# A planned order for an attention, Fourier and feed-forward kernel: small copies on ScalarE's DMA queue, weights loaded and converted in pairs, and the planner's times replaced

## The chip, the cores and the metric

The kernel runs on one core of one Trainium2 chip. The metric is the device time of one execution in microseconds (us). The kernel before takes 1331.78 us, the median of three runs (1328.76 to 1334.36). Engines are named as in the profile: PE (TensorE), PEld (its weight loads), DVE (VectorE), ACT (ScalarE), POOL (GpSimd), SP (SyncE, which here only issues DMAs).

## What is computed

Eight batches of eight heads, 576 positions, head width 64, in float32:

```python
scores = q @ k.T / sqrt(64)                 # block-causal mask, blocks of 64
x = softmax(scores) @ v                     # heads side by side: [8, 576, 512]
u = x + real(fft(fft(x, axis=1), axis=2))   # over positions, then channels
un = (u - mean(u)) / sqrt(var(u) + 1e-6)
out = u + relu(un @ w_ch1) @ w_ch2          # 512 -> 2048 -> 512
```

The weights come as float64, handed over as the 64-bit integers that hold them: 32 rows of 128x512, 512 KB each.

## The kernel before

**Work per head.** Heads are numbered 0 to 63; heads 0 to 7 make batch 0. A head's raw q and k are loaded (`raw`, L288), rounded by ACT into a high part (`lead`, L291), and two DMAs copy parts of `lead` into another tile (`rest`, L295 and L296). DVE and POOL each compute half of the low part (`rest`, L302 and L304). PE then multiplies four pieces whose row maxima DVE reduces (`M`, L382 and L386, combined by L388). A transpose (L195), ACT (`mt`, L397) and a DMA of 2.5 KB (L399, `lead<-mt`) bring the maximum back as one more row of `lead`; this step is called the shift. Only after it landed can the scores run on PE (`rest` and `lead` with 73 rows). ACT takes two exponentials of each scores piece (`ph` L428, `p` L429) and POOL their difference (`pl`, L430). PE multiplies `ph` and `pl` with the two halves of V (`av`); DVE divides (`DEN`, `rec`, then `x` at L468). There is one `av` accumulator in all, so the next head's values wait for the `x` of this one. V arrives once for a pair of heads in a single buffer (`V`, L308), is summed by ACT (L317), and a small product with `ones` on PE (`vacc,ones`) and DVE and ACT split it (`VH` L333, `VL` L334).

**After a batch's eighth head** the results are written to DRAM (`xd`), read back partly mirrored (L529 to L532), folded by DVE (`tmp`, L543 and L544), transformed by 72 matmuls (with `fs`, `zc`, `zs`), normalised (L683 to L688), turned by PE, and then fed through the two weight matrices: 192 matmuls into `h` and 96 into `acc` for each of 18 pairs of pieces. These feed matmuls are most of PE's work and serve as filler between the attention steps of later batches.

**Weights.** Each of 32 rows of weights is loaded by SP (L803) into space of `W` that is not yet used, or into three tiles `u`; DVE makes float32 of it by three instructions of 128x512 (L812, L814, L816), ACT squares and sums (L818). When the sixteen rows of `w_ch1` are through, `weight_scale` finds a scale (a PE product with `ones` and `wst`), and `weight_parts` makes the two half-precision parts (ACT L840 and L843, POOL L844; for `w_ch2` ACT L840, DVE L846). Heads from 8 on may be planned only once the last row of weights has been converted (`"w32"`).

**The order.** `tile_attn_fourier_ffn` holds lanes of `Step`s and plans them with a small model of time: a step has a cost on PE and a chain of stays on the other engines (`"D0.65"` is 0.65 us of DVE, `"Q"` the SP queue, `"L"` a landing); `issue` books these on `Queue`s, adds `HOP` at each hand-over, and the next step emitted is one whose inputs the model calls ready. PE keeps the emitted order; the other engines' order is laid down by the framework when the program is built. Every engine then works strictly in its order.

Of the kernel before, what the change touches and what calls it, by code (L numbers as in the profile page):

```python
# [9 lines left out]
F32 = mybir.dt.float32  # L10
F32R = mybir.dt.float32r
F16 = mybir.dt.float16
# [20 lines left out]

HOP = 0.25
MARGIN = 0.3
AHEAD = (1.5, 6.0)
FREE = 0.5

PSHIFT = 5
# [112 lines left out]
class Queue:  # L152


    def __init__(self):
        self.taken = []

    def fit(self, t, cost):
# [18 lines left out]
def tile_attn_fourier_ffn(  # L177
# [67 lines left out]
    now = 0.0  # L245
    queues = {x: Queue() for x in "DAGQ"}
    done = {}
# [11 lines left out]
    def issue(step):  # L259
        nonlocal current, now  # L260
        t = max(now, ready(step))
        if step.cost:
            now = t = t + step.cost
            for x in queues.values():
                x.forget(now)
        free = None
        for engine, cost in step.chain:
            if engine == "B":
                free = t + HOP
            else:  # L270
                t = t + cost if engine == "L" else queues[engine].book(t + HOP, cost)
# [18 lines left out]
    def lead(h):  # L290
        nc.scalar.copy(LEAD[h % NB][0:D, 64:], raws[h])  # L291

    def lead_copies(h):
        x0, x1 = REST[h % NB].bitcast(F32), LEAD[h % NB].bitcast(F32)
        nc.sync.dma_start(x0[D:P, 0:S], x1[0:D, 64:64 + S])  # L295
        nc.sync.dma_start(x0[0:D, S:], x1[0:D, 64 + S:])  # L296

# [45 lines left out]
    def prepare_lane():  # L343
        for h in range(B * H):
# [3 lines left out]
            )  # L348
            yield Step(lambda: lead_copies(h), 0.0, ("Q1.2", "L2.2"), (("T", h),), ("TC", h), place=h - 0.9)
            yield Step(lambda: rest(h, 0), 0.0, (_d(S),), (("T", h),), ("T2", h, 0), place=h - 0.8)  # L350
# [41 lines left out]
    def shift(h):  # L392

        t = ps_tile()
        tp(t[0:5, 0:P], M[h % 2][:, 0:5], ident)
        mt = work.tile([5, P], F32R, name="mt", bufs=2)
        nc.scalar.activation(mt, t[0:5, 0:P], AF.Copy, bias=float(8.0 * PSHIFT * np.log(2.0)), scale=-1.0)  # L397
        dst = LEAD[h % NB][KM:KS, 0:640].rearrange("r (j p) -> r j p", j=5)
        nc.sync.dma_start(dst.bitcast(F32), mt.bitcast(F32))  # L399

# [87 lines left out]
    def max_lane():  # L488
        for h in range(B * H):
            for n in range(4):  # L490
# [3 lines left out]
                )  # L494
            yield Step(lambda: shift(h), 0.12, ("A0.26", "B", "Q0.6", "L2.2"), (("M", h),), ("X", h), True, place=h - 0.6)

# [281 lines left out]
    wsum = work.tile([P, NK, 2, P], F16, name="ul", bufs=2).rearrange("p c n d -> p (c n d)").bitcast(F32)  # L778
    wjunk = work.tile([P, DM], F32, name="left", bufs=2).bitcast(F16)[:, 0:DM]
    wst = work.tile([P, 8], F32, name="wst")  # L780

    def weight(i):

        if i < NF:
            return w1[P * (i % NK):P * (i % NK + 1), DM * (i // NK):DM * (i // NK + 1)]
        return w2[P * (i - NF):P * (i - NF + 1)]
# [5 lines left out]
    def raw(i):  # L792
        at = LANDS[i]
        t = stage[-1 - at].rearrange("p c d -> p (c d)") if at < 0 else W[:, at:at + 2].rearrange("p i x n -> p (i x n)")
        return t.bitcast(I32)

    loads = [0]

    def weight_loads(n):

        i = loads[0]
        while i < 2 * NF and LANDS[i] not in LANDS[n:i]:
            nc.sync.dma_start(raw(i), weight(i).bitcast(I32))  # L803
            i += 1
        loads[0] = i

    def weight_single(i):
        if loads[0] < i + 2:
            weight_loads(i)
        two = [(raw(j).rearrange("p (n x) -> p x n", x=2), W[:, j + 2].rearrange("p x n -> p (x n)").bitcast(I32)) for j in (i, i + 1)]  # L810
        for r, t in two:
            nc.vector.tensor_scalar(t, r[:, 1], 3, 0x3FFFFFFF, op0=ALU.logical_shift_left, op1=ALU.bitwise_and)  # L812
        for r, t in two:
            nc.vector.scalar_tensor_tensor(t, r[:, 0], 29, t, op0=ALU.logical_shift_right, op1=ALU.bitwise_or)  # L814
        for r, t in two:
            nc.vector.scalar_tensor_tensor(t, r[:, 1], -(1 << 30), t, op0=ALU.bitwise_and, op1=ALU.bitwise_or)  # L816
        for j, (r, t) in enumerate(two):
            nc.scalar.activation(wjunk, t.bitcast(F32), AF.Square, accum_out=wsum[:, i + j:i + j + 1])  # L818
        weight_loads(i)

# [27 lines left out]
    def weight_lane():  # L848
        yield Step(lambda: weight_loads(0), 0.0, ("Q5",), (("L", 0),), ("load",))
        def single(i):  # L850
            return Step(
                lambda: weight_single(i), 0.0, ("D0.5", "D0.5", "D0.82", "D0.82", "D0.85", "D0.85", "A0.82", "A0.82"), (("load",),),
                "w32" if i == 2 * NF - 2 else None,
            )
# [6 lines left out]

        for i in range(0, NF, 2):
            yield single(i)
        yield scale(0)
        for i in range(0, NF, 2):
            yield single(NF + i)
            yield parts(i)
            yield parts(i + 1)
        yield scale(1)
# [116 lines left out]
```

## Time and profile before

| what | us |
|---|---|
| median of three runs | 1331.78 |
| the profiled execution | 1330.52 |
| its span, first to last instruction | 1328.7 |
| PE busy in the span | 1190.9 |
| DVE / ACT / POOL busy | 701.5 / 573.0 / 526.6 |
| last `x` of batch 0 (head 7) starts on DVE at | 139.55 |
| first transform matmul of batch 0 at | 153.39 |

Times of the profile count from the start of the span; about 1.8 us of the profiled execution lie outside it. A busy engine need not be the one that sets the end: what matters is which engine has no idle time left in a stretch, and what the others wait for there.

### The profile page before, as it was taken

What the parts mean: (1) busy time and instruction counts of PE and PEld (TensorE: products, weight loads), DVE (VectorE), ACT (ScalarE), POOL (GpSimd) and SP (SyncE); (2) the same over time, 40 slices, a digit from 0 to 9 for tenths busy, and PEclk for the clock granted to TensorE, in tenths of its full rate; (3) what the DMA queues carried; (4) which work ended last, traced back from release to release, by engine and by line L of the source; (5) the groups of instructions that cost most, each with busy time, mean ns of one, the idle gap of its engine ahead of it and who ended that gap; (6) DMA issues with size and microseconds to landing.
All of it is one profiled execution on the core that took longest, in us unless ns stands there. A gap on an engine that the chain in (4) does not pass through costs nothing.

```text
span 1328.7 us, 25730 instructions
## 1 busy us (share of the span) xinstructions
PE 1190.9 (90%) x10068; PEld 890.2 (67%) x10068; DVE 701.5 (53%) x1626; ACT 573.0 (43%) x1309; POOL 526.6 (40%) x564
## 2 busy tenths in 40 slices
PE   3456469999998999899899899999999999999998
PEld 2455357777676777777677677777767667666665
DVE  6895477465656645764444764567433433312221
ACT  4566566554545454545455645554322112111111
POOL 5455454454544744464454475444601302100000
PEclk9995569999999999999999999999999999999999
DMA  9756212242223224222432323330011000000000
GB/s 296 220 175 186 63 32 67 78 128 59 72 74 98 77 59 123 66 76 73 116 84 64 85 76 94 85 98 24 22 33 37 21 17 21 17 1 17 17 17 16
DMA packets 56167, 99.10 MB, mean 75 GB/s; under 512 B 7933, under 2 KB 26829, under 8 KB 55920
## 3 DMA queue, kind: packets, MB, share of 16 engines
q1 hardware_dynamic: 53760, 89.94, 24.3%
q0 software_dynamic: 2288, 7.54, 1.9%
q8 instruction: 79, 1.29, 0.4%
q14 instruction: 40, 0.33, 0.1%
HBM read 58.46 MB, written 18.87 MB: 58 GB/s over the span
## 4 chain that ended last, share of the span: by engine, by line
PE 71%; DVE 13%; DMA 4%; ACT 4%; POOL 3%; issue 3%; SPq 0%; DVEq 0%; POOLq 0%; ACTq 0%
PE acc L192 25%; PE h L192 24%; PE ps L192 15%; PE av L192 5%; DVE M L386 2%; DVE tmp L543 1%; DMA W<-in_moe_w_ch_dram 1%; PE ps L195 1%; DMA U<-xd,rows 1%; DVE W L814 1%; DVE W L812 1%; DVE W L816 1%; POOL pl L430 1%; POOL u L532 1%; DVE rest L302 1%
## 5 line engine op out<-in xcount | busy, mean ns | idle before, releaser
L192 PE MATMUL h<-uh,W 128*128 128x256 f16 x2304 | 450.8, 275 | 0.0
L430 POOL TENSOR_TENSOR pl<-p,ph 128x288 f16<-128x288 f32 (+1 forms) x256 | 258.5, 1019 | 355.2 <-issue 170.5
L192 PEld LDWEIGHTS <-W 128*128 128x128 f16 x3456 | 324.9, 99 | 88.2 <-issue 5.3
L192 PE MATMUL acc<-W,gh 128*128 128x512 f16 x1152 | 347.4, 383 | 0.0
L192 PE MATMUL h<-ul,W 128*128 128x256 f16 x1152 | 315.7, 274 | 0.1
L738 DVE SCALAR_TENSOR_TENSOR gl<-h,gh 128x256 f16<-128x256 f32 x288 | 120.7, 419 | 305.8 <-ACT gh L737 304.9
L737 ACT ACTIVATE gh<-h 128x256 f16<-128x256 f32 x288 | 110.3, 383 | 381.3 <-PE h L192 375.1
L192 PE MATMUL acc<-W,gl 128*128 128x512 f16 x576 | 220.0, 382 | 1.9 <-DVE gl L738 1.8
L192 PE MATMUL ps<-lead 72*128 72x320 f32 (+5 forms) x711 | 205.1, 347 | 18.5 <-DMA lead<-mt 10.1
L428 ACT ACTIVATE ph<-ps 128x512 f16<-128x512 f32 (+1 forms) x237 | 119.4, 504 | 87.2 <-PE ps L192 85.1
L192 PEld LDWEIGHTS ps<-lead 72*128 72x128 f32 (+1 forms) x711 | 129.5, 202 | 27.5 <-DMA lead<-mt 10.4
L192 PEld LDWEIGHTS <-gh 128*128 128x128 f16 x1152 | 100.3, 100 | 64.7 <-issue 6.8
L386 DVE TENSOR_REDUCE M<-ps 128x1 f32<-128x320 f32 (+2 forms) x239 | 123.5, 528 | 37.7 <-PE ps L192 36.5
L192 PEld LDWEIGHTS <-ph 128*128 128x128 f16 x1920 | 113.8, 104 | 41.0 <-DVE x L468 18.9
L192 PE MATMUL av<-VH,ph 128*128 128x65 f16 x960 | 119.0, 203 | 20.2 <-DVE x L468 8.9
L192 PE MATMUL av<-VH,pl 128*128 128x65 f16 x960 | 117.3, 201 | 19.1 <-POOL pl L430 19.0
L192 PE MATMUL ps<-rest 128*128 128x288 f32 (+1 forms) x354 | 125.1, 360 | 2.8 <-ACT p L429 1.3
L429 ACT ACTIVATE p<-ps 128x512 f32<-128x512 f32 (+1 forms) x237 | 119.4, 504 | 6.2 <-POOL pl L430 6.0
L192 PE MATMUL av<-VL,ph 128*128 128x64 f16 x960 | 118.2, 200 | 0.0
L304 POOL TENSOR_TENSOR rest<-raw,lead 64x576 fp32r<-64x576 f32 x64 | 111.2, 1738 | 17.7 <-ACT lead L291 13.4
L192 PEld LDWEIGHTS <-pl 128*128 128x128 f16 x960 | 94.4, 103 | 21.8 <-POOL pl L430 21.3
L192 PEld LDWEIGHTS <-gl 128*128 128x128 f16 x576 | 56.6, 98 | 74.0 <-DVE gl L738 5.5
(172 smaller groups left out, 1391.3 us busy)
## 6 DMA issues: line engine op xcount, KB each, us to landing
raw<-in_qk_dram SPq DMA_DIRECT2D x64, 288.0 KB
rest<-lead SPq DMA_DIRECT2D x128, 144.0 KB
W<-in_moe_w_ch_dram SPq DMA_DIRECT2D x24, 512.0 KB
V<-in_v_dram SPq DMA_DIRECT2D x32, 320.0 KB
xd<-x SPq DMA_DIRECT2D x32, 256.0 KB
out_dram<-u SPq DMA_DIRECT2D x32, 256.0 KB
u<-in_moe_w_ch_dram SPq DMA_DIRECT2D x8, 512.0 KB
u<-xd SPq DMA_DIRECT2D x8, 512.0 KB
```

Source lines behind the costliest of these rows:

```text
L192: return tc.keep_in_program_order(nc.tensor.matmul(*args, **kw))
L195: return tc.keep_in_program_order(nc.tensor.transpose(*args, **kw))
L302: nc.vector.tensor_tensor(x0[0:D, 0:S], raw[:, 0:S], x1[0:D, 64:64 + S], op=ALU.subtract)
L304: nc.gpsimd.tensor_tensor(x0[D:P, S:], raw[:, S:], x1[0:D, 64 + S:], op=ALU.subtract)
L386: nc.vector.tensor_reduce(m[:, j:j + 1], t[:, at - hi:at], axis=AX.X, op=ALU.max)
L428: nc.scalar.activation(ph[:, at:at + w], t[:, 0:w], AF.Exp, scale=0.125)
L429: nc.scalar.activation(p32[:, 0:w], t[:, 0:w], AF.Exp, scale=0.125)
L430: nc.gpsimd.tensor_tensor(pl[:, at:at + w], p32[:, 0:w], ph[:, at:at + w], op=ALU.subtract)
L532: nc.gpsimd.indirect_dma_start(dst, None, xd, bass.IndirectOffsetOnAxis(ap=rows[0:dst.shape[0], i:i + 1], axis=0))
L543: nc.vector.tensor_tensor(e[0:r], X[c][0:r], U[c][0:r], op=op)
L737: nc.scalar.activation(gh, t, AF.Relu)
L738: nc.vector.scalar_tensor_tensor(gl, t, 0.0, gh, op0=ALU.max, op1=ALU.subtract)
```

## The change

Four things are changed.

1. **Queue.** For heads 0 to 7 the two copies into `rest` and the shift's DMA are issued from ACT's DMA queue (`quick(h)`), for all later heads from SP as before.
2. **Pairs.** Weights are loaded two rows at a time (1 MB) into four places of `W` (18, 22, 26, 30), at most three loads past the one in work (`FLIGHT`); DVE's three instructions and ACT's square take both rows at once (128x1024). Of the 32 rows 28 go in 14 pairs. The last four stay single and pass through the `u` tiles. POOL clears the sum of each pair's second row.
3. **Planner's times.** `HOP` goes from 0.25 to 0.05, with 0.2 more after a step on PE; a booking on an engine is shorter than the stay by a tail (`TAIL`), so that the next may start before the result is handed over. The chains name ACT instead of the SP queue for the copies of heads 0 to 7.
4. **Order of the weight lane.** The scale of `w_ch1` follows its last pair; after each pair of `w_ch2` come the parts of as many rows of `w_ch1`.

```diff
-HOP = 0.25
+HOP, FROM_PE = 0.05, 0.2
+TAIL = {"A": 0.11, "D": 0.08, "G": 0.03, "Q": 0.0}
+FLIGHT = 3
...
     def book(self, t, cost):
+        cost -= self.tail
         t = self.fit(t, cost)
         self.taken.append((t, t + cost))
         self.taken.sort()
-        return t + cost
+        return t + cost + self.tail
...
         free = None
+        if step.cost:
+            t += FROM_PE
         for engine, cost in step.chain:
...
+    def quick(h):
+        return nc.scalar if h < H else nc.sync
+
     def lead_copies(h):
         x0, x1 = REST[h % NB].bitcast(F32), LEAD[h % NB].bitcast(F32)
-        nc.sync.dma_start(x0[D:P, 0:S], x1[0:D, 64:64 + S])
-        nc.sync.dma_start(x0[0:D, S:], x1[0:D, 64 + S:])
+        quick(h).dma_start(x0[D:P, 0:S], x1[0:D, 64:64 + S])
+        quick(h).dma_start(x0[0:D, S:], x1[0:D, 64 + S:])
...
-        nc.sync.dma_start(dst.bitcast(F32), mt.bitcast(F32))
+        quick(h).dma_start(dst.bitcast(F32), mt.bitcast(F32))
...
-    LANDS = [(18, 20, 22, 24)[i % 4] for i in range(NF)]
-    LANDS += [26, 28, 30, 32, -1, -2, -3, 26, 28, 30, 32, -1, -2, -3, -1, -2]
+    LANDS = [(2 * k, 2, x) for k, x in enumerate((18, 22, 26, 30, 18, 22, 26, 30, 22, 26, 30, 26, 30, 30))]
+    LANDS += [(28 + k, 1, x) for k, x in enumerate((-1, -2, -3, -1))]
...
+        while x < len(LANDS) and x < done + FLIGHT and LANDS[x][2] not in [y[2] for y in LANDS[done:x]]:
+            i, n, at = LANDS[x]
+            nc.sync.dma_start(raw(x).rearrange("p (j n) -> p j n", j=n), weight(i, n))
+            x += 1
...
+        i, n, at = LANDS[x]
+        r = raw(x).rearrange("p (n x) -> p x n", x=2)
+        t = W[:, i + 2:i + 2 + n].rearrange("p i x n -> p (i x n)").bitcast(I32)
+        nc.vector.tensor_scalar(t, r[:, 1], 3, 0x3FFFFFFF, op0=ALU.logical_shift_left, op1=ALU.bitwise_and)
+        nc.vector.scalar_tensor_tensor(t, r[:, 0], 29, t, op0=ALU.logical_shift_right, op1=ALU.bitwise_or)
+        nc.vector.scalar_tensor_tensor(t, r[:, 1], -(1 << 30), t, op0=ALU.bitwise_and, op1=ALU.bitwise_or)
+        nc.scalar.activation(wjunk[:, 0:DM * n], t.bitcast(F32), AF.Square, accum_out=wsum[:, i:i + 1])
+        if n == 2:
+            nc.gpsimd.memset(wsum[:, i + 1:i + 2], 0.0)
```

In the listings of the order below, a row is one instruction (x4: four alike), with out<-in and the size of what it writes; numbers behind a name tell buffers apart, so `lead0`, `lead1`, `lead2` serve heads 0, 1, 2, then 3, 4, 5 and so on, and `M_0`, `M_1` even and odd heads.

**SP's queue at the start**, from the first weight load on. Before:

```order
L803 DMA W_114<-in_moe_w_ch1_dram 128x1024 x4
L295 DMA rest0_87<-lead0_84 64x576
L296 DMA rest0_87<-lead0_84 64x576
L288 DMA raw_165<-in_qk_dram 64x1152
L295 DMA rest1_88<-lead1_85 64x576
L296 DMA rest1_88<-lead1_85 64x576
L288 DMA raw_192<-in_qk_dram 64x1152
L803 DMA W_114<-in_moe_w_ch2_dram 128x1024 x3
L399 DMA lead0_84<-mt_173 1x5x128
L803 DMA W_114<-in_moe_w_ch2_dram 128x1024
L803 DMA W_114<-in_moe_w_ch1_dram 128x1024
```

After:

```order
L819 DMA W_114<-in_moe_w_ch1_dram 128x2x1024 x4
L296 DMA raw_164<-in_qk_dram 64x1152
L296 DMA raw_191<-in_qk_dram 64x1152
L819 DMA W_114<-in_moe_w_ch1_dram 128x2x1024
L320 DMA V_193<-in_v_dram 128x640
L819 DMA W_114<-in_moe_w_ch1_dram 128x2x1024 x2
L296 DMA raw_366<-in_qk_dram 64x1152
L819 DMA W_114<-in_moe_w_ch1_dram 128x2x1024
L296 DMA raw_506<-in_qk_dram 64x1152
L819 DMA W_114<-in_moe_w_ch2_dram 128x2x1024 x2
L296 DMA raw_580<-in_qk_dram 64x1152
```

The copies `rest<-lead` and the shift `lead<-mt` are gone from SP, and 1 MB loads of weights alternate with the loads of raw heads and of V.

**ACT at the start**, from the first `lead`. Before:

```order
L291 CAST lead0_84<-raw_122 64x1152
L317 ACTIVATE tmp_130,vacc_129<-V_124 128x640
L291 CAST lead1_85<-raw_126 64x1152
L397 ACTIVATE mt_173<-acc_171 5x128
L818 ACTIVATE left_120,ul_119<-W_114 128x512
L333 ACTIVATE VH_0_94<-V_124,vacc_129 128x10x64
L818 ACTIVATE left_120,ul_119<-W_114 128x512
L291 CAST lead2_86<-raw_165 64x1152
L818 ACTIVATE left_120,ul_119<-W_114 128x512
L397 ACTIVATE mt_198<-h_196 5x128
```

After:

```order
L299 CAST lead0_84<-raw_122 64x1152
L329 ACTIVATE tmp_130,vacc_129<-V_124 128x640
L307 DMA rest0_87<-lead0_84 64x576
L308 DMA rest0_87<-lead0_84 64x576
L299 CAST lead1_85<-raw_126 64x1152
L307 DMA rest1_88<-lead1_85 64x576
L308 DMA rest1_88<-lead1_85 64x576
L409 ACTIVATE mt_172<-acc_170 5x128
L411 DMA lead0_84<-mt_172 1x5x128
L345 ACTIVATE VH_0_94<-V_124,vacc_129 128x10x64
L832 ACTIVATE left_120,ul_119<-W_114 128x1024
L409 ACTIVATE mt_197<-h_195 5x128
```

The six DMAs of heads 0 and 1 now stand between ACT's computations. In the new program every DMA of SP and ACT together takes one of eight completion semaphores in turn, and waits for the DMA that had it before; so the second `rest1` copy waits for the first weight load, and the shift of head 0 (the first `lead0<-mt`) for the third.

**DVE around the maximum of head 6** (`M_0<-M_0`, the combining instruction) and the `x` of head 4. Before, the twelve rows right behind that instruction, down to the `x` of head 4 (`x_859`):

```order
L816 SCALAR_TENSOR_TENSOR W_114<-u_117,W_114 128x512
L816 SCALAR_TENSOR_TENSOR W_114<-u_118,W_114 128x512
L467 RECIPROCAL rec_861<-DEN_0_92 128x5
L328 TENSOR_SCALAR pw_866<-vacc_822 128x1
L884 TENSOR_SCALAR dft_83<-DEN_0_92 1x1
L302 TENSOR_TENSOR rest2_89<-raw_872,lead2_86 64x576
L382 TENSOR_REDUCE M_1_91<-ps_918 128x2
L386 TENSOR_REDUCE M_1_91<-ps_918 128x1
L386 TENSOR_REDUCE M_1_91<-h_924 128x1
L386 TENSOR_REDUCE M_1_91<-acc_931 128x1
L386 TENSOR_REDUCE M_1_91<-acc_934 128x1
L468 TENSOR_TENSOR x_859<-av_806,rec_861 128x5x64
```

After, that instruction among them, and `x_857` the `x` of head 4:

```order
L829 TENSOR_SCALAR W_114<-W_114 128x1024
L314 TENSOR_TENSOR rest1_88<-raw_674,lead1_85 64x576
L398 TENSOR_REDUCE M_0_90<-ps_807 128x1
L830 SCALAR_TENSOR_TENSOR W_114<-W_114 128x1024
L346 SCALAR_TENSOR_TENSOR VL_1_97<-V_602,vacc_732,VH_1_95 128x640
L400 TENSOR_TENSOR M_0_90<-M_0_90 128x1
L831 SCALAR_TENSOR_TENSOR W_114<-W_114 128x1024
L477 TENSOR_SCALAR DEN_0_92<-av_811,vacc_476 128x5
L479 RECIPROCAL rec_859<-DEN_0_92 128x5
L902 TENSOR_SCALAR dft_83<-DEN_0_92 1x1
L480 TENSOR_TENSOR x_857<-av_811,rec_859 128x5x64
```

The `x` of head 4 was the twelfth row behind the maximum of head 6; now it is the fifth. Of the weights' instructions 88 of 128x512 stand ahead of that maximum before (30 of L812, 30 of L814, 28 of L816), and 41 of 128x1024 now (14, 14, 13). The last four rows of weights now stand on DVE behind the `x` of head 7, three of them (but for one instruction) ahead of the first fold of batch 0:

```order
L479 RECIPROCAL rec_1240<-DEN_1_93 128x5
L480 TENSOR_TENSOR x_1139<-av_1184,rec_1240 128x5x64
L829 TENSOR_SCALAR W_114<-u_116 128x512
L830 SCALAR_TENSOR_TENSOR W_114<-u_116,W_114 128x512
L831 SCALAR_TENSOR_TENSOR W_114<-u_116,W_114 128x512
L829 TENSOR_SCALAR W_114<-u_117 128x512
L830 SCALAR_TENSOR_TENSOR W_114<-u_117,W_114 128x512
L831 SCALAR_TENSOR_TENSOR W_114<-u_117,W_114 128x512
L829 TENSOR_SCALAR W_114<-u_118 128x512
L830 SCALAR_TENSOR_TENSOR W_114<-u_118,W_114 128x512
L555 TENSOR_TENSOR tmp_1271<-X2_1248,U2_1247 33x512
L555 TENSOR_TENSOR tmp_1282<-u_1245,u_1246 128x512
```

Their four loads stand on SP behind the reading back of `xd`.

More of the change, by code (lines that the diff above doesn't have):

```diff
@@ L795, in raw @@
+    LANDS = [(2 * k, 2, x) for k, x in enumerate((18, 22, 26, 30, 18, 22, 26, 30, 22, 26, 30, 26, 30, 30))]
+    LANDS += [(28 + k, 1, x) for k, x in enumerate((-1, -2, -3, -1))]
+    def raw(x):
+        i, n, at = LANDS[x]
+        t = stage[-1 - at].rearrange("p c d -> p (c d)") if at < 0 else W[:, at:at + 4].rearrange("p i x n -> p (i x n)")
         return t.bitcast(I32)
     loads = [0]
[L799 to L805, printed above, removed]
@@ L860, in parts @@
             return Step(lambda: weight_parts(i), 0.0, ("A1.45", "G1.2") if i < NF else ("A0.73", "D0.75"), (("scale", i // NF),), ("w", i))
[L862 to L868, printed above, removed]
+        for x in range(len(LANDS)):
+            i, n, at = LANDS[x]
+            yield single(x)
+            if i == NF - 2:
+                yield scale(0)
+            if i >= NF:
+                for j in range(n):
+                    yield parts(i - NF + j)
         yield scale(1)
```

50 lines of the change are left out of this document (23 added, 27 removed).

## The prediction

> **What bounds the kernel now.** I read the page first, then busy times by stretches, then the waits and the timeline of the first 180 us. From the page (digits are tenths of a slice of 33 us):
>
> ```profile
> span 1328.7 us, 25730 instructions
> PE 1190.9 (90%) x10068; PEld 890.2 (67%) x10068; DVE 701.5 (53%) x1626; ACT 573.0 (43%) x1309; POOL 526.6 (40%) x564
> PE   3456469999998999899899899999999999999998
> PEclk9995569999999999999999999999999999999999
> ```
>
> The PE row has two parts: six slices in which PE is half empty, then a stretch in which it is nearly full to the end. By stretches (start to end, length, then busy us and count by engine, granted clock, DMA share, GB/s):
>
> ```profile
> 0.00:46.00 46.00, 17.22 (x97) 14.83 (x98) 29.70 (x67) 19.96 (x43) 21.19 (x20) 1.00 0.98 293
> 46.00:116.00 70.00, 37.23 (x316) 31.51 (x316) 68.67 (x144) 41.01 (x99) 35.39 (x23) 0.85 0.67 201
> 116.00:140.00 24.00, 13.87 (x119) 12.32 (x119) 5.49 (x16) 19.61 (x38) 17.62 (x16) 0.50 0.32 89
> 140.00:182.00 42.00, 21.52 (x111) 16.67 (x112) 24.72 (x59) 19.02 (x38) 17.79 (x25) 0.64 0.14 39
> 182.00:211.00 29.00, 23.31 (x193) 18.59 (x192) 23.51 (x49) 22.89 (x47) 15.74 (x15) 0.76 0.21 54
> 211.00:1000.00 789.00, 753.67 (x6990) 572.68 (x6989) 452.82 (x1080) 390.51 (x895) 387.65 (x415) 0.98 0.29 76
> 1000.00:1328.70 328.70, 324.06 (x2250) 223.65 (x2248) 96.57 (x215) 60.03 (x153) 31.17 (x52) 1.00 0.06 18
> ```
>
> To 46 us the DMA engines are full (0.98) and DVE idles 46 - 29.7 = 16.3 us. To 116 us DVE is full (68.67 of 70). From 116 to 140 nothing is; there the last two heads of batch 0 run through one behind the other. To 182 comes the latency of the first transform, and from 211 on PE: its idle time there is 35.3 us up to 1000, and 4.6 us after. PE's work is the same before and after the change. So each us by which the first 182 us shorten should come off the end, and a change of the 35.3 us adds to it.
>
> **The change, step by step.** I follow four points of the early chain: the maximum of head 6 on DVE, the scores of head 6, the `x` of head 7, the first transform matmul. The rows of the first three, with what held them up:
>
> ```profile
> 101.93 0.14 DVE L388 TENSOR_TENSOR M<-M 128x1 f32<-128x1 f32 x1
> 107.08 0.47 DVE L468 TENSOR_TENSOR x<-av,rec 128x320 f32<-128x320 f32 x1
> 111.35 0.34 SPq L308 DMA_DIRECT2D V<-in_v_dram  x1
> 118.07 0.74 ACT L317 ACTIVATE tmp<-V 128x640 f16<-128x640 f32 x1 [3.27 <-DMA V<-in_v_dram]
> 118.95 0.58 PE L192 MATMUL h<-vacc,ones 128*128 128x1 f32 x2 [6.59 <-ACT tmp L317]
> 119.40 0.59 PE L192 MATMUL h<-rest 128*128 128x288 f32 x1
> 139.55 0.49 DVE L468 TENSOR_TENSOR x<-av,rec 128x320 f32<-128x320 f32 x1
> ...
> dft<-in_c_dft_dram POOLq DMA_DIRECT2D x1, 2606.0 KB, 11.4
> ```
>
> *DVE's work ahead of the maximum of head 6.* The weights' instructions up to 116 us (busy us, mean ns):
>
> ```profile
> L816 DVE SCALAR_TENSOR_TENSOR W<-W 128x512 int32<-128x512 int32 x24 | 17.1, 721 | 0.1
> L814 DVE SCALAR_TENSOR_TENSOR W<-W 128x512 int32<-128x512 int32 x24 | 16.0, 676 | 0.2
> L812 DVE TENSOR_SCALAR W<-W 128x512 int32<-128x512 int32 x24 | 13.2, 557 | 9.2 <-DMA W<-in_moe_w_ch_dram 9.2
> L814 DVE SCALAR_TENSOR_TENSOR W<-u,W 128x512 int32<-128x512 int32 x8 | 7.9, 993 | 0.0
> L816 DVE SCALAR_TENSOR_TENSOR W<-u,W 128x512 int32<-128x512 int32 x8 | 5.9, 744 | 0.0
> L812 DVE TENSOR_SCALAR W<-u 128x512 int32<-128x512 int32 x8 | 4.2, 540 | 1.2 <-DMA u<-in_moe_w_ch_dram 1.2
> ```
>
> Together 64.3 us for 32 rows, 2.0 us a row. By the two orders 30, 30 and 28 rows' worth stand ahead of that maximum before, and 28, 28 and 26 after: two rows less, 4.0 us. In pairs an instruction's fixed part is paid once for two rows. No 128x1024 instruction is in the trace; what the fixed part is, these rows bound:
>
> ```profile
> L386 DVE TENSOR_REDUCE M<-ps 128x1 f32<-128x512 f32 x53 | 35.7, 673 | 6.8 <-PE ps L192 6.7
> L386 DVE TENSOR_REDUCE M<-ps 128x1 f32<-128x192 f32 x53 | 18.2, 344 | 0.0
> 69.16 1.28 DVE L814 SCALAR_TENSOR_TENSOR W<-W 128x512 int32<-128x512 int32 x2
> ```
>
> 320 columns more cost 329 ns, so 512 cost 0.53 us. The second of two L814 adds 1.28 - 0.67 = 0.61 us, hence 0.08 us fixed; a lone 512 (0.673) would say 0.14, and a wide instruction without gain says 0. I take 0.08, since DVE's instructions follow each other closely here: 41 x 0.08 = 3.3 us (0 to 5.7). Sum of this step 7.3 us (4.0 to 9.7).
>
> *Waiting for weights and shifts.* The L812 row shows 9.2 us of DVE's idle time as waits for weight loads, all before 46 us. Beside it PE waits for a shift (head 1):
>
> ```profile
> 22.28 0.27 ACT L397 ACTIVATE mt<-h 5x128 fp32r<-5x128 f32 x1 [0.99 <-PE h L195]
> 30.07 0.77 SPq L399 DMA_DIRECT2D lead<-mt  x1
> 40.07 0.61 PE L192 MATMUL ps<-lead 73*128 73x288 f32 x1 [10.06 <-DMA lead<-mt]
> 32.06 0.52 SPq L295 DMA_DIRECT2D rest<-lead  x1
> 32.67 0.55 SPq L296 DMA_DIRECT2D rest<-lead  x1
> ```
>
> Its DMA is ready at 22.55, issued at 30.07 behind SP's weight loads, and used at 40.07, 17.5 us in all for 2.5 KB. On ACT's queue the 7.5 us until issue go (its semaphore is that of a `rest` copy, not of a load), and the 10 us in flight shrink if the transfer needn't stand behind megabytes. Scores that come earlier don't shorten DVE's full stretch, but give DVE maxima and rests to do while it waits for weights. I take half of the 9.2 us, 4.6 (0 to 9.2). The Trainium skill has two rules on this in its page "DMA: Bandwidth & Descriptors". By the section "Queues, rings and completion order" each DMA engine goes round between the queues packet by packet, which speaks for a shorter flight; by "Issuing engines are not separate DMA queues" DMAs of all engines run on the same 16 DMA engines, so that another queue saves issue time alone, and with that the term would be 0 and the sum 16.8. No row here shows a small DMA on a second queue beside a full one, so the trace doesn't decide between them.
>
> ACT pays for the issues: per head 0.52 + 0.55 + 0.77, for eight heads 14.7 us. ACT is busy 80.6 of the first 140 us, so idle time covers it, unless the issue itself waits (a rival below). SP loses 24 of its issues and 14 weight loads; it only issues. POOL's 14 clears of one column fall into its idle time ahead of the first `rest`. ACT's squares of 128x1024 save ACT time that isn't wanted there.
>
> *From the maximum to the scores of head 6:* 17.5 us before. Two waits lie in it. The `x` of head 4 comes 5.2 us after the maximum, and only then can the single `av` take head 5's values. And PE stands 6.59 us at V's small product until 118.95, since V's load, issued at 111.35 beside the 2.6 MB of transform tables, lands only at 118. After, one wide weight instruction and three small ones lie between the maximum and that `x` (2 x 0.67 - 0.08 = 1.3, and some tenths: about 2 us), then 45 value matmuls; V's load is issued ahead of the tables', and its product stands behind the scores. ACT still sums V ahead of head 6's exponentials. I take 6 us for the step, so 11.5 us won (6.5 if V again takes 6.6 us to land and holds ACT; 13.5 if only the shift's own DMA remains).
>
> *From the scores of head 6 to the `x` of head 7:* 20.2 us. Twelve instead of eight of ACT's weight parts now stand ahead of head 7's last exponential, at
>
> ```profile
> L840 ACT ACTIVATE W<-W,wst 128x512 f16<-128x512 f32 x9 | 6.3, 712 | 0.1
> ```
>
> about 4 x 0.7 = 2.8, and the shift of 0.8; against that the scale stands a little earlier in PE's order. I take a loss of 2 (0 to 3.6).
>
> *The late rows of weights.* Four rows move behind head 7 on DVE, their loads behind the mirrored reading. Before, DVE is free there:
>
> ```profile
> 149.04 0.88 DVE L543 TENSOR_TENSOR tmp<-X,U 33x512 f32<-33x512 f32 x1 [9.00 <-DMA U<-xd,rows]
> ```
>
> The 9 us of waiting cover the eight instructions that stand ahead of the fold, if three loads land within it. The third row's last instruction and the fourth row's three stand between the folds: 0.744 + 0.540 + 0.993 + 0.744 = 3.0 us by the `u` rows. I take a loss of 3 (0 if they fill gaps, 6 if the loads land 3 us late).
>
> *The rest of the order.* All steps after batch 0 are planned anew. PE's waits from 200 to 1000 us are few and long:
>
> ```profile
> PE av L192 <- POOL pl L430: 8.5, 7, 3.4
> PE ps L192 <- DVE M L386: 7.8, 6, 2.7
> ```
>
> The stays in the planner now follow the trace more closely, and in the new order the last value matmul is PE's 6838th instead of its 7484th matmul of 10034, so the stretch in which PE can stall is a tenth shorter: a tenth of 35.3 us, I take a gain of 3 (from 14 lost to 16 won: some two fifths of the 35.3 either way, as a new order can make such waits or remove them).
>
> Sum: 7.3 + 4.6 + 11.5 - 2 - 3 + 3 = 21.4 us, of which 18.4 come before the first transform. Against the profiled execution (1330.5 us, of which 1328.7 are its span) that is 1309.1 us; the median of the runs is 1.3 higher, so 1310.4, and I say 1310.
>
> **Rivals.**
> 1. *Transfers land no sooner.* The queues share DMA engines that are full, DVE waits for weights as before, and the 4.6 us stay: 1315. For it the share of 0.98 up to 46 us; against it the 7.5 us before the issue, which aren't flight. (The Trainium skill's "Issuing engines are not separate DMA queues" would have it so.)
> 2. *ACT becomes the early bound.* It works strictly in order, and an issue that waits for a weight load holds exponentials and squares. Five issues follow a load on their semaphore. On SP such waits were
>
> ```profile
> SPq L803 <- DMA W<-in_moe_w_ch_dram: 7.0, 7, 2.2
> ```
>
> (total, times, longest). At the longest, 5 x 2.2 = 11, and with 6 of the 14.7 us of issues uncovered, 17 us go: 1327, no change. For it: ACT busy 19.61 of 24 us from 116 to 140. Against: 41.01 of 70 in the stretch that DVE sets.
> 3. *The new order stalls PE.* Values are placed nearer to their scores: counted in the orders after the first transform, the median is 43 matmuls between them, 51 before. POOL and ACT have then less time for `ph` and `pl`. There are 56 x 3 = 168 uses; at 0.15 us more of waiting each (25 us) the 18.4 us are lost and 6.7 more, which is 0.5% slower; at 0.2 us it takes 1331.8 - 18.4 + 33.6 = 1347. Against it: such waits were 7 in number, and POOL is busy 387.65 of 789.
> 4. *The denser order also takes the long waits out*, some 16 us of the 35.3 instead of 3: 1297. For it: few waits make most of the 35.3; against it: nothing in the change aims at DVE's backlog, which the second row names.
>
> **Chances and range.** Likeliest case 0.50, its own range 1302 to 1319; rival 1 0.12; rival 2 0.14; rival 3 0.11; rival 4 0.13. What a measurement tells from no change is about 0.5%, 1325 to 1338. Faster 0.75 (the likeliest, 1, 4), the same 0.14 (2), slower 0.11 (3). The range takes in the bounds above on both sides, rival 2 and most of rival 4, and leaves out rival 3: 1293 to 1330.
>
> **What would show it.** Right: the maximum of head 6 near 90 us, its scores near 96, the `x` of head 7 near 118, the first transform matmul near 135, and PE's idle time from there on at 32 to 36 us. PE's wait for `lead<-mt` of 10 us is gone. Wrong: ACT idle ahead of DMA issues for more than 10 us (rival 2); many PE waits on `pl` under 1 us (rival 3); DVE waiting behind the `x` of head 7 for `u<-in_moe_w_ch_dram` longer than 12 us.

## The result, and the profile after

The changed kernel takes 1352.72 us (median of four runs, 1349.61 to 1355.98) against 1330.81 us before: the ratio is 1.0156, 95% interval 1.0129 to 1.0183. The forecast was 1310. The profiled execution took 1349.61 us. Its page, and busy times by the stretches shown for the kernel before (start to end, length, busy us and count of PE, PEld, DVE, ACT and POOL, then granted clock, DMA share, GB/s):

```profile
span 1347.5 us, 25628 instructions
PE 1195.8 (89%) x10068; PEld 892.5 (66%) x10068; DVE 702.2 (52%) x1584; ACT 561.0 (42%) x1281; POOL 531.4 (39%) x578
PE   2674368989979989999999999999999999999998
PEclk9998678999989999999999999999999999999999
...
0.00:46.00 46.00, 17.05 (x93) 14.27 (x93) 34.49 (x57) 21.04 (x38) 27.29 (x34) 1.00 0.87 266
46.00:116.00 70.00, 46.50 (x362) 40.18 (x363) 57.32 (x107) 40.04 (x84) 37.44 (x28) 1.00 0.64 200
116.00:140.00 24.00, 6.01 (x80) 5.02 (x77) 4.49 (x9) 19.41 (x34) 20.13 (x20) 0.66 0.40 113
140.00:182.00 42.00, 19.84 (x98) 15.06 (x98) 32.67 (x70) 15.25 (x35) 11.17 (x18) 0.62 0.16 56
182.00:211.00 29.00, 25.72 (x228) 19.29 (x225) 24.79 (x51) 21.67 (x43) 13.27 (x12) 0.88 0.21 54
211.00:1000.00 789.00, 738.17 (x6844) 562.60 (x6842) 448.94 (x1071) 380.88 (x890) 391.53 (x417) 0.98 0.29 76
1000.00:1347.50 347.50, 342.52 (x2377) 236.05 (x2375) 99.45 (x222) 62.67 (x160) 30.58 (x52) 1.00 0.06 17
```

Up to 116 us the change does much of what it was to do: DVE is no longer full (57.32 of 70 us, 68.67 before) and PE has done more. From 116 to 140 us PE is idle for 18 of 24. From 211 to 1000 us PE's idle time is 50.8 us where it was 35.3. Behind 1000 us PE is as full as before, only that 18.8 us more are left to do. The early chain, row by row (DVE, PE and ACT; in brackets the idle time ahead and what ended it):

```profile
96.24 0.14 DVE L400 TENSOR_TENSOR M<-M 128x1 f32<-128x1 f32 x1
96.52 0.41 PE L201 MATMUL h<-ident,M 128*5 128x128 f32 x1
101.56 0.26 ACT L409 ACTIVATE mt<-h 5x128 fp32r<-5x128 f32 x1
102.78 0.59 PE L198 MATMUL ps<-rest 128*128 128x288 f32 x1
108.56 0.61 PE L198 MATMUL ps<-lead 73*128 73x288 f32 x1 [5.20 <-DMA lead<-mt]
129.76 0.23 PE L198 MATMUL av<-VH,pl 128*128 128x65 f16 x1 [6.49 <-POOL pl L442]
132.29 0.49 DVE L480 TENSOR_TENSOR x<-av,rec 128x320 f32<-128x320 f32 x1
142.58 0.43 DVE L829 TENSOR_SCALAR W<-u 128x512 int32<-128x512 int32 x1 [9.80 <-DMA u<-in_moe_w_ch_dram]
148.61 0.68 DVE L555 TENSOR_TENSOR tmp<-X,U 33x512 f32<-33x512 f32 x1
152.94 0.61 PE L198 MATMUL ps<-dft,fs 128*128 128x290 f32 x1 [21.17 <-ACT fs L523]
```

The maximum of head 6 is 5.7 us earlier than before and the first matmul of its scores 16.6 us earlier, at 102.78. That one does not need the shift; the second does, and comes only at 108.56. PE has turned the maximum at 96.52, but ACT, which works in its order, makes `mt` of it only at 101.56, behind a square of weights, head 5's exponentials and a `lead`. Then the gain is given back: 5.20 us for the shift's DMA, 6.49 us for `pl`, and 9.80 us in which DVE waits behind the `x` of head 7 for a late row of weights. The first transform matmul comes 0.45 us earlier than before. As the span grew by 18.8 us (1328.7 to 1347.5), 19.2 us are lost behind that matmul. There PE's own waits, from 211 us on, are, among others (total, times, longest):

```profile
PE av L198 <- POOL pl L442: 25.8, 18, 6.6
PE ps L198 <- ACT p L441: 6.7, 6, 2.4
PE acc L198 <- DVE gl L750: 3.4, 5, 1.6
```

Waits of the values for `pl` are 25.8 us, 8.5 before. The longest of them, with POOL's rows ahead of it and the stretch of 8 us behind its start:

```profile
382.97 1.12 POOL L544 DMA_INDIRECT u<-xd,rows  x1 [1.87 <-DMA xd<-x]
384.38 0.98 POOL L544 DMA_INDIRECT u<-xd,rows  x1 [0.30 <-issue]
385.67 0.89 POOL L544 DMA_INDIRECT U<-xd,rows  x1 [0.30 <-issue]
386.63 1.39 POOL L316 TENSOR_TENSOR rest<-raw,lead 64x576 fp32r<-64x576 f32 x1
388.10 1.16 POOL L442 TENSOR_TENSOR pl<-p,ph 128x512 f16<-128x512 f32 x1
...
389.31 0.23 PE L198 MATMUL av<-VH,pl 128*128 128x65 f16 x1 [6.64 <-POOL pl L442]
...
386.00:394.00 8.00, 4.69 (x26) 2.54 (x27) 2.63 (x6) 1.22 (x3) 3.59 (x5) 0.57 0.55 166
```

Three gathers of the mirrored reading, the first of them waiting for `xd`, and half a `rest` stand on POOL ahead of the `pl` that PE wants. The hand-over itself is short: `pl` ends at 388.10 + 1.16 = 389.26, PE starts at 389.31. And the stall costs more than its own length: the granted clock is 0.57 in the 8 us around its end, so PE also works slower behind it.

### The profile page after: what moved, and what is told of

It is laid out like the page before. It is cut to its first block, busy times and chain, and to the rows that moved or that the text cites. A ratio compares the mean times of both kernels' runs of the same rounds, so it can differ in the third digit from the quotient of the medians.

```text
span 1347.5 us, 25628 instructions
## 1 busy us (share of the span) xinstructions
PE 1195.8 (89%) x10068; PEld 892.5 (66%) x10068; DVE 702.2 (52%) x1584; ACT 561.0 (42%) x1281; POOL 531.4 (39%) x578
## 3 DMA queue, kind: packets, MB, share of 16 engines
q10 hardware_dynamic: 1360, 2.38, 0.6%
## 4 chain that ended last, share of the span: by engine, by line
PE 62%; DVE 11%; ACT 7%; DMA 6%; issue 5%; POOL 4%; SPq 0%; DVEq 0%; POOLq 0%; ACTq 0%
PE acc L198 23%; PE h L198 21%; PE ps L198 12%; PE av L198 4%; POOL pl L442 2%; ACT lead L299 2%; ACT ph L440 2%; DVE M L398 2%; DVE tmp L555 1%; ACT p L441 1%; DVE rest L314 1%; DMA lead<-mt 1%; DMA xd<-x 1%; PE ps L201 1%; DMA U<-xd,rows 1%
## 5 line engine op out<-in xcount | busy, mean ns | idle before, releaser
L198 PE MATMUL ps<-lead 73*128 73x288 f32 (+5 forms) x708 | 201.0, 348 | 17.2 <-DMA lead<-mt 7.8
L198 PEld LDWEIGHTS <-gh 128*128 128x128 f16 x1152 | 103.2, 99 | 67.2 <-issue 6.7
L198 PEld LDWEIGHTS ps<-lead 73*128 73x128 f32 (+1 forms) x708 | 128.7, 203 | 26.9 <-DMA lead<-mt 9.2
L198 PE MATMUL ps<-rest 128*128 128x288 f32 (+2 forms) x353 | 125.4, 363 | 7.5 <-ACT p L441 3.7
L316 POOL TENSOR_TENSOR rest<-raw,lead 64x576 fp32r<-64x576 f32 x64 | 114.2, 1785 | 31.6 <-ACT lead L299 23.0
```

Source lines behind the costliest of these rows:

```text
L198: return tc.keep_in_program_order(nc.tensor.matmul(*args, **kw))
L316: nc.gpsimd.tensor_tensor(x0[D:P, S:], raw[:, S:], x1[0:D, 64 + S:], op=ALU.subtract)
```

## How the runs are read

To see where each kernel loses, I weigh every matmul by the median start-to-start time of its kind behind 211 us in all traces (1139 us in sum) and note when 50 us of that work are done (in the kernels before and after about when the first feed matmuls begin; in e1 and e8 some 17 us ahead of them), and how long the next 200 us of work take. In this second stretch stand PE's idle time and the half-clock loss (one minus the granted clock, summed over windows of 1 us; where PE idles at half clock, both count). All numbers in us; ratios are to the kernel before.

| kernel | median | ratio, 95% interval | 50 us done at | next 200 us take | PE idle | half-clock loss | rest to the last matmul |
|---|---|---|---|---|---|---|---|
| before | 1330.8 to 1332.3 | | 178.6 | 220.8 | 13.7 | 9.4 | 925.0 |
| after | 1352.7 | 1.0156 (1.0129 to 1.0183) | 180.3 | 239.0 | 26.0 | 14.4 | 924.1 |
| e1 after, old times | 1330.6 | 0.9997 (0.9976 to 1.0018) | 170.1 | 226.3 | 18.1 | 11.9 | 929.9 |
| e2 before, new times | 1359.1 | 1.0219 (1.0186 to 1.0251) | 180.6 | 242.7 | 27.1 | 15.6 | 929.8 |
| e3 after, SP's queue | 1345.4 | 1.0100 (1.0061 to 1.0140) | 168.3 | 246.3 | 27.9 | 22.0 | 925.3 |
| e4 after without pairs | 1357.3 | 1.0204 (1.0183 to 1.0225) | 185.0 | 238.4 | 21.4 | 18.1 | 927.7 |
| e5 pairs alone | 1342.8 | 1.0089 (1.0058 to 1.0120) | 167.2 | 234.4 | 19.9 | 21.4 | 934.9 |
| e6 ACT's queue alone | 1335.0 | 1.0029 (1.0009 to 1.0049) | 178.2 | 225.8 | 15.2 | 13.8 | 925.2 |
| e7 before, new HOP | 1349.1 | 1.0135 (1.0098 to 1.0171) | 175.0 | 238.9 | 24.0 | 21.8 | 930.5 |
| e8 before, tails | 1335.9 | 1.0048 (1.0028 to 1.0068) | 169.8 | 232.6 | 22.5 | 15.4 | 925.1 |
| e9 after, MARGIN 0.9 | 1326.4 | 0.9954 (0.9931 to 0.9976) | 181.7 | 216.3 | 10.7 | 7.4 | 924.6 |
| e10 e3, MARGIN 0.9 | 1318.7 | 0.9897 (0.9862 to 0.9932) | 167.8 | 219.6 | 13.9 | 9.3 | 924.4 |
| e11 e3, MARGIN 1.5 | 1313.9 | 0.9860 (0.9831 to 0.9890) | 165.3 | 229.7 | 17.7 | 16.8 | 912.9 |
| e12 before, HOP 0.24 | 1330.1 | 0.9990 (0.9970 to 1.0010) | 185.4 | 218.2 | 12.1 | 7.8 | 923.0 |
| e13 before, MARGIN 0.9 | 1334.2 | 1.0004 (0.9977 to 1.0031) | 179.3 | 224.9 | 11.4 | 14.5 | 923.1 |
| e14 before, MARGIN 1.5 | 1345.6 | 1.0095 (1.0079 to 1.0112) | 181.0 | 260.8 | 25.1 | 38.4 | 899.1 |
| e15 e3, MARGIN 2.5 | 1343.9 | 1.0098 (1.0072 to 1.0124) | 164.7 | 251.3 | 23.0 | 32.1 | 920.0 |
| e16 e11, early last rows | 1311.2 | 0.9849 (0.9820 to 0.9877) | 164.7 | 227.1 | 19.5 | 11.0 | 911.1 |
| e17 e10, early last rows | 1316.5 | 0.9887 (0.9860 to 0.9914) | 161.8 | 221.7 | 15.1 | 11.2 | 922.1 |

For the changed kernel: the stretch of 200 us of work takes 18.3 us more, of which 12.3 are idle time and 5.0 half clock. Before it and behind it the two kernels are within 2 us of each other.

## Experiments: the planner's times

e1 undoes the new times in the changed kernel, e2 does them alone; e7 and e8 split them; e12 is the smallest change of them.

```diff
-HOP, FROM_PE = 0.05, 0.2                                     # e1, in after
-TAIL = {"A": 0.11, "D": 0.08, "G": 0.03, "Q": 0.0}
+HOP, FROM_PE = 0.25, 0.0
+TAIL = {"A": 0.0, "D": 0.0, "G": 0.0, "Q": 0.0}
...
-HOP = 0.25                                                   # in before
+HOP, FROM_PE = 0.05, 0.2; TAIL as in after                   # e2
+HOP, FROM_PE = 0.05, 0.2; TAIL all 0.0                       # e7
+HOP, FROM_PE = 0.25, 0.0; TAIL as in after                   # e8
+HOP = 0.24                                                   # e12
```

> The changed kernel with the planner's old times (HOP 0.25, nothing added after PE, no tails); queue, pairs and lane order stay new. Theory A (the new times let the planner place consumers on PE before their inputs are there: the 14 us of extra PE idle time between 211 and 421 us and the half-clock stretches behind it): PE's idle time from 211 to 1000 us falls from 50.8 to about 35, and the time to about 1332. Theory B (the last weight rows, late behind head 7, bunch the first heads of batch 1): the stalls stay, about 1352. Theory C (each new plan is a draw of lots, and the stalls are not tied to any part): anywhere between 1325 and 1360.

> The kernel before with the planner's new times alone. Theory A: the stalls come with the times, PE's idle time from 211 to 1000 us rises from 35 to about 50, time about 1350. Theory B: no stalls without late rows, about 1331. Theory C: anywhere between 1325 and 1360, with stalls in other places than in the changed kernel.

> The kernel before with HOP 0.05 and 0.2 after PE, without the tails. Theory A1 (the shorter hand-over does the harm: each step from engine to engine is planned 0.2 us sooner): about 1350 to 1359, as with all new times (1359.1). Theory A2 (the tails do it: the planner takes ACT, DVE and POOL to be free sooner than they are): about 1331.

> The kernel before with the tails alone (ACT 0.11, DVE 0.08, POOL 0.03 us), HOP 0.25, nothing added after PE. Theory A1: about 1331. Theory A2: about 1350 to 1359. Both in part: each some 1340.

> The kernel before with HOP 0.24 instead of 0.25, a change too small to mean anything: it shows how far two plans lie apart by themselves. If plans are a draw (theory C): some 5 to 20 us off 1331. If the order follows the times smoothly: within 4 us.

With the old times the loss is gone (1330.6), and PE's idle time from 211 to 1000 us falls from 50.8 to 38.9 us (35 were expected). The new times alone cost 28 us (1359.1), more than the whole change, and that idle time rises from 35.3 to 54.2. The hop alone costs 18, the tails alone 4 to 5; that both together cost more than the sum is 6 us, which the intervals do not separate from nothing. Theory B falls: e2 has no late rows and stalls as much. Theory C does too in its plain form, as HOP 0.24 moves the time by 1.6 us against the kernel before of the same runs. In e2 the values wait for `pl` more than before, as in the changed kernel: 17.9 us against 8.5, which is half of the idle time that is added (the stretch, then PE's longest group of waits from 211 to 1000 us):

```profile
211.00:421.00 210.00, 185.58 (x1785) 143.73 (x1785) 134.84 (x304) 113.70 (x263) 112.79 (x117) 0.98 0.33 88
...
PE av L196 <- POOL pl L436: 17.9, 16, 3.0
```

Behind a scores piece the planner counts four hand-overs (two on ACT, one on POOL, one at the end): 4 x 0.25 = 1.0 us before, 0.2 + 4 x 0.05 = 0.4 now. The 0.6 us less are true of the hand-over (0.05 us in the row above) and still too little, since the model does not see all that holds a queue. In the longest wait above, the planner books 3 us of POOL for the gathers as soon as the last values are through, but nothing for the landing of `xd`, at which POOL stands for 1.87 us. That the other waits for `pl` have a like reason was not followed.

One pair speaks against the new times as the whole cause: with pairs and the copies on SP, the old times take 1342.8 us (e5, below) and the new ones 1345.4 (e3), only 2.6 more, where the other three pairs differ by 22 to 28.

## Experiments: slack given back

If the old hop was a margin in disguise, an open margin must do the same. MARGIN is how long an attention step must have been ready in the model before it goes ahead of ready feed work.

```diff
-MARGIN = 0.3
+MARGIN = 0.9      # e9 in after; e10 in e3 (below); e13 in before
+MARGIN = 1.5      # e11 in e3; e14 in before
+MARGIN = 2.5      # e15 in e3
```

> The changed kernel with MARGIN 0.9 instead of 0.3 (a step of attention is taken ahead of ready feed work only when the planner has held it ready for 0.9 us). Theory D (the old HOP held about 0.6 us of unspoken slack between a scores piece and its values, which the planner's model needs; the new times took it away): PE's idle time between 180 and 420 us falls from 26 to about 17, time about 1340. Rival (the slack is not what matters, each plan is a draw): about 1350, or anything from 1335 to 1360.

> The same with the small copies on SP's queue as well (pairs and new times stay). Theory D: the 10 us won in the first 170 us stay and the stalls shrink: about 1330. Rival (an early start makes attention denser behind it, and PE's stalls and half-clock stretches give the gain back whatever the margin): about 1342.

> As the run before with MARGIN 1.5. Theory D: no worse than with 0.9, about 1325 to 1332. Rival: about 1342.

> The kernel before with MARGIN 0.9, nothing else. If the old HOP held the slack that the planner needs and no more is useful, a wider margin on top of it brings little: within 5 us of 1331. If any slack is worth having, PE's idle time behind 180 us falls and the time is about 1318 to 1322, and the gain of the kernels with MARGIN 0.9 and 1.5 was the margin's and not that of pairs and an early start.

> The kernel before with MARGIN 1.5. As the run before: within 5 us of 1331 if the old HOP sufficed, about 1315 to 1320 if slack of itself is what the kernel with 1313.9 gained.

> Pairs and new times, small copies on SP, MARGIN 2.5: where the slack becomes too much. If the stalls between 170 and 420 us go on shrinking: 1305 to 1311. If attention is now delayed and its tail is no longer covered: 1316 or more.

Theory D holds, and by more than expected: one number takes 26 us off the changed kernel (1352.7 to 1326.4), its idle time in the stretch falls from 26.0 to 10.7 us and the half-clock loss from 14.4 to 7.4. With the early gain of e3 it comes to 1318.7, and with MARGIN 1.5 to 1313.9. The first stretch is e9's, the other two rows e11's:

```profile
211.00:421.00 210.00, 199.47 (x1892) 153.71 (x1891) 124.13 (x302) 111.24 (x255) 111.22 (x114) 0.97 0.33 88
...
211.00:421.00 210.00, 197.33 (x1858) 150.49 (x1857) 120.77 (x286) 106.97 (x242) 106.44 (x110) 0.97 0.31 84
1000.00:1312.00 312.00, 307.35 (x2130) 212.05 (x2127) 91.87 (x205) 56.74 (x145) 30.86 (x52) 1.00 0.06 17
```

It is not a gain of the margin itself: on the old hop, without pairs, 0.9 brings nothing (1334.2) and 1.5 loses (1345.6), as 2.5 does on the new one (1343.9). So there is a best amount of slack. With pairs on ACT's queue the old hop does almost as well as the margin (1330.6 in e1, 1326.4 in e9); with pairs on SP's queue it does not (1342.8 in e5, against 1318.7 and 1313.9). Too much slack fails in a way that I had not looked for. In e14, stretch by stretch:

```profile
211.00:421.00 210.00, 190.09 (x1615) 145.90 (x1613) 111.20 (x265) 100.83 (x222) 97.76 (x99) 0.85 0.28 76
...
380.00:400.00 20.00, 14.16 (x124) 12.17 (x121) 13.58 (x29) 10.61 (x20) 16.27 (x21) 0.59 0.36 90
```

From 211 to 421 us PE is idle for 19.9 us, less than in the changed kernel, but the granted clock is 0.85; the half-clock loss of the table is 38.4 us.

## Experiments: the queue and the pairs

```diff
     def quick(h):
-        return nc.scalar if h < H else nc.sync
+        return nc.sync                     # e3; the chains say Q again
```

e5 is e3 with the old times, so pairs and lane order alone. e6 is the kernel before with `quick` and the chains of the change, and e4 that with the new times as well.

> The changed kernel with the small copies of heads 0 to 7 and the shift back on SP's queue, and the planner told so. If the queue is worth its 7.5 us of issue time, x of head 7 comes later than its 132.3 us, at about 139; the end stays near 1352 in theories A and B, since the late rows hold the first fold at about 149 us in any case. Theory C: 1325 to 1360.

> The kernel before with ACT's queue and the new planner's times, weights in single rows and in the old lane order. Theory A: stalls as in the changed kernel, about 1345 to 1350. Theory B: no late rows, no stalls, first fold some 5 us earlier than 149.0: about 1326. Theory C: 1325 to 1360.

> Weights in pairs and the new lane order alone: planner's old times, small copies on SP's queue. The kernel with pairs, ACT's queue and old times took 1330.6. If ACT's queue costs what it costs under the new times (x of head 7 at 132.3 with it, at 116.8 without; 7 us of the end), this one takes about 1322, with x of head 7 near 118. If the queue is worth its issue time, as the prediction had it, x of head 7 comes later than 132 and the time is about 1335.

> The kernel before with ACT's queue for the small copies of heads 0 to 7 alone (the planner told so). If the queue is worth its issue time: x of head 7 some 5 us before 139.6, time about 1326. If ACT stands at its DMA issues behind weight loads: x of head 7 later by 5 us or more, time about 1337.

My expectation for e3 was the wrong way round. On SP's queue the maximum of head 6 comes at 84.81 us, 11.4 us before that of the changed kernel, the `x` of head 7 at 116.83, 15.5 us before, and the first transform matmul at 141.30, 11.6 us before. 50 us of PE's work are done 12 us sooner:

```profile
84.81 1.10 DVE L400 TENSOR_TENSOR M<-M 128x1 f32<-128x1 f32 x1
...
93.14 0.76 SPq L411 DMA_DIRECT2D lead<-mt  x1
...
100.62 0.61 PE L198 MATMUL ps<-lead 73*128 73x288 f32 x1 [5.83 <-DMA lead<-mt]
...
116.83 0.49 DVE L480 TENSOR_TENSOR x<-av,rec 128x320 f32<-128x320 f32 x1
...
141.30 0.61 PE L198 MATMUL acc<-dft,fs 128*128 128x290 f32 x1 [25.00 <-ACT fs L523]
```

The shift of head 6 is issued at 93.14 and used at 100.62, 7.5 us; on ACT's queue it was issued at 101.85 and used at 108.56, 6.7 us. The queue hardly shortens the flight. What ACT's queue costs shows first at the first shift of the changed kernel (ACT, then DVE, then the shift of head 6):

```profile
12.49 0.27 ACT L409 ACTIVATE mt<-acc 5x128 fp32r<-5x128 f32 x1 [2.52 <-PE acc L201]
19.32 1.28 ACTq L411 DMA_DIRECT2D lead<-mt  x1
20.65 0.83 ACT L345 ACTIVATE VH<-V,vacc 128x640 f16<-128x640 f32 x1 [7.89 <-issue]
...
21.52 0.89 DVE L346 SCALAR_TENSOR_TENSOR VL<-V,vacc,VH 128x640 f16<-128x640 f32 x1 [4.45 <-ACT VH L345]
101.85 0.74 ACTq L411 DMA_DIRECT2D lead<-mt  x1
```

ACT is through with `mt` at 12.76 and stands 7.89 us at the issue, whose semaphore is that of the third weight load; DVE then waits 4.45 us for ACT. From there to head 6 the two orders differ in much else, so that not every one of the 11.4 us is shown to come from this stand. The Trainium skill's page "DMA: Bandwidth & Descriptors" (section "Issuing engines are not separate DMA queues") has DMAs of all engines on the same 16 DMA engines; the two flights, 6.7 and 7.5 us, agree with it.

At the end the queue is worth less and not always of one sign. SP's is better by 7.4 us under the new times (after against e3), by 7.8 with MARGIN 0.9 (e9 against e10) and by 3.5 without pairs (e6 against the kernel before of its runs, with the `x` of head 7 at 139.53 and so where it was). Without pairs and with the new times the `x` of head 7 comes at 140.20 on ACT's queue (e4) and at 134.69 on SP's (e2), while the ends are within 2 us. Under the old times ACT's is better by 12.3 (e1 against e5), although e5 is 2.9 us ahead at the first 50 us of work: it loses 8.1 in the next 200 and 5.0 behind them. Much of that is half clock: its loss is 21.4 us against 11.9 in the table, and one piece of half clock lasts 20.5 us, from 336.3 us on. Neither of the two times expected for e5, 1322 and 1335, came, although the `x` of head 7 did come early, at 120.34. Why this one plan runs into that stretch is open; no second plan near it was tried. So a plan as a whole still scatters by some 10 us, more than HOP 0.24 shows.

## Experiments: the last four rows of weights

In e11 the `x` of head 7 comes at 114.31, and yet the first transform starts only 24.2 us later, where it was 13.84 in the kernel before:

```profile
114.31 0.49 DVE L480 TENSOR_TENSOR x<-av,rec 128x320 f32<-128x320 f32 x1
126.05 0.72 DVE L829 TENSOR_SCALAR W<-u 128x512 int32<-128x512 int32 x1 [11.24 <-DMA u<-in_moe_w_ch_dram]
...
133.30 1.63 DVE L555 TENSOR_TENSOR tmp<-X,U 33x512 f32<-33x512 f32 x1
...
138.52 0.61 PE L198 MATMUL acc<-dft,fs 128*128 128x290 f32 x1 [24.73 <-ACT fs L523]
```

e16 (on e11) and e17 (on e10) write three of the four late loads right behind the tenth pair's load (the expectation says ahead of it). `put(x)` issues load x. In the order they then stand among the first loads, and all late rows are converted ahead of the last two `x`.

```diff
-            i, n, at = LANDS[x]
-            nc.sync.dma_start(raw(x).rearrange("p (j n) -> p j n", j=n), weight(i, n))
+            if x < 14 or x == 17:
+                put(x)
+            if x == 9:
+                for y in (14, 15, 16):
+                    put(y)
```

> The kernel with 1313.9 (pairs, new times, copies on SP, MARGIN 1.5) with the loads of the last rows into the u tiles written ahead of the tenth pair's load, so that the last rows are converted before the x of head 6 and nothing stands ahead of the first fold. If the late rows hold the fold (DVE waits 11.2 us for their load there, and the fold comes 19.0 us after the x of head 7 where 9.5 would do): fold at about 128, nine or ten microseconds less before the first transform of which some may be lost behind it: 1304 to 1310. If 1.5 MB more at the start delays the pairs by as much: 1314.

> The same on the kernel with MARGIN 0.9 (1318.7). If the late rows hold the fold: 1309 to 1315. If not: 1319.

By the medians they gain 2.7 and 2.2 us, where 4 to 10 were expected. By the ratios it is 0.0011 and 0.0010, less than the intervals, so no gain is shown for certain. In e16:

```profile
120.19 0.49 DVE L480 TENSOR_TENSOR x<-av,rec 128x320 f32<-128x320 f32 x1
131.03 2.44 DVE L555 TENSOR_TENSOR tmp<-X,U 33x512 f32<-33x512 f32 x1 [10.36 <-DMA U<-xd,rows]
...
136.92 0.61 PE L198 MATMUL acc<-dft,fs 128*128 128x290 f32 x1 [17.26 <-ACT fs L523]
```

From the `x` of head 7 to the fold it is 10.8 us now instead of 19.0, but that `x` itself comes 5.9 us later, as DVE now does the rows ahead of it, and the first transform is 1.6 us earlier. By its median e16 is the best kernel of the study: 1311.2 us, 0.9849 of the kernel before.

## Why the prediction was wrong

**The step that failed** is "the rest of the order", put at a gain of 3 us, because "the stays in the planner now follow the trace more closely" and the last value matmul comes earlier. It was a loss of 19.2 us, outside the 14 of its lower bound, and the reason was wrong in both halves. Stays that follow the trace more closely leave out a slack that the plan lived on (e1, e2, e9). And the earlier last value (6838th matmul; also in e2) is no gain: it runs at 878.9 us where it ran at 955.6, so the same attention steps are packed into a shorter time, and PE waits more in it. In the three kernels with MARGIN 0.9 on the new times it is the 7232nd matmul, with 1.5 the 7881st. The rival "the new order stalls PE" named the place (values waiting for `pl`) and the nearer distance (43 matmuls against 51), and had a chance of 0.11. It was sized as many waits of 0.15 us; it came as 18 waits with a longest of 6.6, and with half clock behind them, which no term had. The range, too, was narrower than the terms: with each at its own lower bound they add up to a loss of 13 us, some 1345, and the range ended at 1330.

**Up to the first transform** 18.4 us were forecast and 0.45 came, a miss almost as large. The term that failed first is the queue: ACT's issues were taken to be covered by idle time and to save waits, but with the same pairs and times on SP (e3) the maximum of head 6 is 17.1 us earlier than before instead of 5.7, and the first transform 12.1 us earlier instead of 0.45. Step by step:
- The maximum of head 6: 11.9 us forecast for the first two steps, 5.7 measured. The merging gave less than thought (a pair takes 1423 + 1422 + 910 = 3755 ns, two single rows 2 x 1954 = 3908: 0.05 us a merge instead of 0.08), the waits for weights fell by more (10.4 to 2.0 us), and ACT at its issue, on which DVE waited in turn for 4.45 us, took a part back. The forecast counted ACT's issues and gave waiting issues to a rival.
- From there to the scores of head 6: 6.5 us, forecast 6. That is right only for the first matmul; to the second, which needs the shift, it is 12.3 us, since ACT came late to `mt`. In the kernel before, the two stood 0.4 us apart. So the agreement is luck, and the rest of this step falls into the next one.
- From the scores to the `x` of head 7: 29.5 us, a loss of 9.4 where 2 was taken (0 to 3.6): the shift's flight of 5.20 us that PE now meets, and the wait of 6.49 for `pl`, while ACT and POOL work on weight parts between head 7's exponentials.
- From that `x` to the first transform: 20.65 us instead of 13.84, a loss of 6.8 where 3 was taken (0 to 6). The loads, issued behind the mirrored reading and waited for 9.80 us, land when the old wait would have ended (142.58 is 10.3 us behind the `x`, the fold before was 9.5), so the 9 us cover none of the eight instructions: all 6.0 us of them stand bare ahead of the fold.

**What held:** PE's wait of 10 us for the shift of head 1 is gone, and pairs bring PE's first 50 us of work forward by 11 to 12 us (e5 against before, e3 against e2). That the kernels with the slack back and the copies on SP take 1311 to 1319 us (e10, e11, e16, e17), near the forecast of 1310, is in part luck. They have a margin that the forecast did not know, and some of their gain lies elsewhere (e11 wins 12 us behind the first 250 us of work). No run has the margin and the new times without pairs, so the share of the pairs in it is not shown.

## What to carry to other kernels

A planner's constant that is larger than the measured hand-over can be its safety margin: replace it by the measured value and the margin has to be put back by name, with a size found by trying more than one. A single plan can still come out 10 us off (e5), so one run of one plan decides little. Before small DMAs go to a computing engine's queue, look at which earlier DMA each must wait for; the engine stands still meanwhile. And a stall of PE is to be priced with the half clock behind it.

## What the runs showed of the hardware that I had not expected

Short waits lower PE's clock. In the kernel before, a wait of 1.96 us is followed by 3.41 us at half clock (PE, then the stretch with the wait and the one behind it):

```profile
340.41 0.28 PE L195 MATMUL ps<-ident,M 128*5 128x128 f32 x1 [1.96 <-DVE M L388]
...
337.39:340.80 3.41, 1.45 (x12) 0.98 (x10) 3.31 (x7) 0.08 (x1) 3.17 (x4) 1.00 0.39 89
340.80:344.21 3.41, 3.41 (x26) 2.55 (x26) 2.02 (x6) 0.19 (x1) 2.09 (x4) 0.50 0.27 83
```

In all nineteen traces the granted clock changes only at the steps of a fixed grid of 3.41 us, so it matters how much of one such stretch PE is idle. Of the stretches at full clock in which PE was busy for less than 0.4 of the time, all 118 were followed by half clock; between 0.4 and 0.6 it was 73 of 126, and above 0.85 none of 5669. So a longer wait that falls across two stretches can pass: in the changed kernel one of 2.38 us, up to 295.24 us, leaves PE busy for 1.79 and 2.40 us of two stretches of 3.41, and no half clock follows.

The Trainium skill's page "TensorE: Matmul & The Clock Gate" (section "Part 1: The HAM clock gate (the "warmup" mystery)") gives the fall to half rate after an idle window of about 3.4 us, and the rise after a busy one. Here waits of less than that bring it about (1.96 us in the row above), so the measurement differs on the first; the length of the short dips fits the second. What a stall costs is thus not its own length: in e14 20 us at a mean clock of 0.59 go by with PE busy for 14.16 of them.
